# Rebuilding the opening of an attention and SwiGLU kernel: loads ahead of constants, idle matmuls at the start, product with V and row sums ahead of the scores

## The chip, the cores and the metric

The kernel runs on one core of a Trainium2 chip. The metric is the device time of one execution in microseconds (us). A profile is one execution taken by the hardware profiler; its span is about 1.7 us shorter than the time of the same run.

## The reference

Block-sparse attention (4 batches, 8 heads, 768 positions, head size 64) feeds an RMS norm and a SwiGLU layer (3072 tokens, 512 wide, 1536 hidden). Cut to what matters:

```python
scores = (q @ k.T) / sqrt(64)                     # per batch and head
mask = window of one 32-block | first and last block | three sampled blocks per block row
attn = exp(where(mask, scores, -1e9) - max); attn = attn / sum(attn)
x = (attn @ v)                                    # to (3072, 512)
xn = x / sqrt(mean(x * x) + 1e-6) * rms_g
out = (silu(xn @ w_gate) * (xn @ w_val)) @ w_out
```

## The kernel before

A step is one third of a head pair in one half of a batch: two score tiles (128 keys x 2 heads x 384 queries), their exponentials on ScalarE, and the mask multiplications on VectorE. There are 96 steps; the pair n has the steps 3n to 3n+2, and four pairs (12 steps) make a unit u. In step 3n+4 follow the product of the probabilities with V (`av`) and the row sums (`zsum`). When a unit has its four pairs, norm matmuls follow, and then its FFN, cut into pieces of 0.65 us of TensorE time (`ff_g`, `ff_v`, `ff_y`). A loop deals the pieces out to the steps of the next unit: every step earns a credit, `rate`, and each thing placed costs its entry. The order in which the Python emits instructions is the order in each engine's queue. The score tiles share two PSUM buffers (tag "s"), and so does the output of `av` from pair 8 on.

```python
    load_qk(0, 0, 2)                      # q, k of the first pair of heads
    ident = const.tile([P, P], BF16, name="ident")
    nc.vector.memset(ident, 0.0)
    # ... Bm (32x32), Kind (32x768): memsets on VectorE; then on GpSimd ident, jb and seven
    # ... affine_selects that shape Bm and Kind ...
    load_qk(0, 2, 4)
    load_v(0)
    load_qk(0, 4, 8)
    # ... casts and three scalar_tensor_tensors on VectorE put the sampled blocks into Bm ...
    transposes(0, 0)
    # ... Ez, Ew, Sel, SelB, FHL, nhalf on GpSimd ...
    load_w()                              # w_gate, w_val
    # ...
    def qk_mm(n, jt):
        u, pr = divmod(n, NP)
        b, ic = divmod(u, 2)
        if jt == 0:
            ptiles[n] = ppool.tile([P, NC, 2, TG], BF16, name="pt", tag="pt")
        s_ = ps_s.tile([P, 2, 512], FP32, name="s_", tag="s")
        x = qk[b]
        for e in range(2):
            nc.tensor.matmul(
                out=s_[:, e, 0:TG],
                lhsT=x[64 * e:64 * e + 64, 1, jt, pr, :],
                rhs=x[64 * e:64 * e + 64, 0, ic * NT:(ic + 1) * NT, pr, :],
                start=True, stop=True)
        return s_

    def exp_(n, jt, s_):
        nc.scalar.activation(
            out=ptiles[n][:, jt, :, :], in_=s_[:, :, 0:TG], func=AF.Exp, scale=SCALE)

    def mask_(n, jt):
        ic = (n // NP) % 2
        pv = ptiles[n][:, jt]
        nc.vector.tensor_tensor(
            out=pv, in0=pv,
            in1=Mk[:, jt, ic * TG:(ic + 1) * TG].unsqueeze(1).to_broadcast([P, 2, TG]),
            op=ALU.mult)

    def av(n, shared):
        u, pr = divmod(n, NP)
        b = u // 2
        pt_, vb = ptiles[n], vtiles[b]
        if pr == 0:
            osb[u] = opool.tile([P, NP, TG], FP32, name="osb", tag="osb")
            o2s[u] = work.tile([P, NP, TG], BF16, name="o2", tag="o2")
            zwt[u] = ps_a.tile([P, 512], FP32, name="zw", tag="zw")[:, 0:TG]
        if shared:
            o_ = ps_s.tile([P, 2, 512], FP32, name="o_", tag="s")[:, 0, 0:TG]
        else:
            o_ = ps_a.tile([P, 512], FP32, name="oa", tag="acc")[:, 0:TG]
        for jt in range(NC):
            for e in range(2):
                nc.tensor.matmul(
                    out=o_[64 * e:64 * e + 64, :],
                    lhsT=vb[:, 2 * pr + e, jt * D:(jt + 1) * D],
                    rhs=pt_[:, jt, e, :], start=(jt == 0), stop=(jt == NC - 1),
                    skip_group_check=True)
        nc.scalar.copy(out=osb[u][:, pr, :], in_=o_)
        (nc.vector if u == 0 else nc.gpsimd).tensor_tensor(
            out=o2s[u][:, pr, :], in0=osb[u][:, pr, :], in1=osb[u][:, pr, :], op=ALU.mult)

    def zsum(n):
        u, pr = divmod(n, NP)
        pt_ = ptiles[n]
        for j2 in range(NC // 2):
            for e in range(2):
                for par in range(2):
                    c = 2 * e + par
                    nc.tensor.matmul(
                        out=zwt[u][32 * c:32 * c + 32, :], lhsT=Ez[:, pr, :],
                        rhs=pt_[:, 2 * j2 + par, e, :],
                        start=(pr == 0 and j2 == 0), stop=False, skip_group_check=True)

    def ff_g(u, f, wide):
        if f == 0:
            hps[u] = ffw.tile([P, NF, TG], BF16, name="hp", tag="hp", bufs=2)
        if wide:
            gp = ps_s.tile([P, 2, 512], FP32, name="gw", tag="s")[:, 0, 0:TG]
        else:
            gp = ps_f.tile([P, TG], FP32, name="gp", tag="gp")
        for c in range(NP):
            nc.tensor.matmul(
                out=gp, lhsT=wg[:, c, f * P:(f + 1) * P], rhs=xns[u][:, c, :],
                start=(c == 0), stop=(c == NP - 1))
        th = ffw.tile([P, TG], BF16, name="th", tag="th")
        nc.scalar.activation(out=th, in_=gp, func=AF.Tanh, scale=0.5)
        uu = ffw.tile([P, TG], BF16, name="uu", tag="uu")
        nc.vector.scalar_tensor_tensor(
            out=uu, in0=th, scalar=1.0, in1=gp, op0=ALU.add, op1=ALU.mult)
        gst[(u, f)] = uu
    # ... ff_v and ff_y in the same way: four matmuls and a product on VectorE; three matmuls,
    # ... and after every fourth ff_y an output copy on ScalarE and a store ...

    for n in range(NU * NP):
        u, pr = divmod(n, NP)
        s1 = 3 * (n + 1)
        at(s1 + 1, 1.25, av, n, n >= 8)
        at(s1 + 1, 0.7, zsum, n)
        if pr == NP - 1:
            when = (2, 3, 4, 5, 6, 6) if u == 0 else (2, 3, 4, 5, 6, 8)
            at(s1 + when[0], 0.4, norm_a, u)
            at(s1 + when[1], 0.6, norm_b, u)
            at(s1 + when[2], 0.0, norm_c, u)
            at(s1 + when[3], 0.3, norm_d, u)
            at(s1 + when[4], 0.35, norm_e, u, 0)
            at(s1 + when[5], 0.35, norm_e, u, 1)
    for pr in range(1, NP):
        at(3 * (pr - 1) + 1, 0.95, transposes, 0, pr)
    at(1, 0.3, mask_query, 0)
    at(1, 0.3, mask_build, 0, 0, 4)
    at(2, 0.3, mask_build, 0, 4, 6)
    at(5, 0.3, mask_query, 1)
    for i in range(3):
        at(6 + i, 0.3, mask_build, 1, 2 * i, 2 * i + 2)
    for b in range(1, B):
        base = 24 * (b - 1)
        for c in range(NC):
            for i in range(2):
                at(base + (7 + c if b == 1 else 1 + 2 * c + i), 0, load_c, b, i, c)
        for i in range(2):
            at(base + 17, 0, transposes_dma, b, i)
        at(3 * (8 * (b - 1) + (4 if b == 1 else 5)) + 1, 0, load_v, b)
    at(13, 0, load_wo)
    # ...
    while True:
        if step in starts:
            u = starts.index(step)
            queue += ffq[u]
            if u == 0:
                credit = 0.0
        since = 0.0
        todo = fixed.pop(step, ())
        if step < NSTEP:
            n, j = divmod(step, NC // 2)
            sa = qk_mm(n, 2 * j)
            exp_(n, 2 * j, sa)
            sb = qk_mm(n, 2 * j + 1)
            if step < 2:
                exp_(n, 2 * j + 1, sb)
                late += [(n, 2 * j), (n, 2 * j + 1)]
            else:
                for m in late:
                    mask_(*m)
                late = [(n, 2 * j), (n, 2 * j + 1)]
                if queue:
                    since += feed()
                exp_(n, 2 * j + 1, sb)
            credit -= QKT
        else:
            for m in late:
                mask_(*m)
            late = []
        if todo:
            while queue and since < 0.6 and step < NSTEP:
                since += feed()
        tail = 0.0
        for cost, fn, a in todo:
            fn(*a)
            credit -= cost
            if fn in (transposes, norm_d, norm_e):
                tail = 1.2
        while queue and tail > 0 and step < NSTEP:
            c = feed()
            tail -= c
            since += c
        credit -= since
        if u >= 0:
            credit += rate.get(u, 99.0)
            keep = RESERVE if step < NSTEP else 0
            while len(queue) > keep and credit > 0:
                credit -= feed()
            if len(queue) <= keep:
                credit = min(credit, 0.0)
        step += 1
```

The softmax here doesn't subtract the row's maximum and nothing guards it: scores larger than these inputs give would overflow.

Of the kernel before, what the change touches and what calls it, by code (L numbers as in the profile page):

```python
# [17 lines left out]
def kernel(  # L18
# [12 lines left out]
    nc = tc.nc  # L31
# [51 lines left out]
    def load_v(b):  # L83
# [11 lines left out]
    load_qk(0, 0, 2)  # L95


    ident = const.tile([P, P], BF16, name="ident")
    nc.vector.memset(ident, 0.0)
# [6 lines left out]
    nc.gpsimd.affine_select(  # L106
        out=ident, in_=ident, compare_op=ALU.not_equal, fill=1.0,
        base=0, pattern=[[-1, P]], channel_multiplier=1)
# [18 lines left out]
    load_qk(0, 2, 4)  # L127
    load_v(0)
    load_qk(0, 4, 8)

    wg = const.tile([P, DM // P, DFF], BF16, name="wg")
    wv = const.tile([P, DM // P, DFF], BF16, name="wv")
    wo = const.tile([P, NF, DM], BF16, name="wo")
    wgv = moe_w_gate.rearrange("(c p) f -> p c f", p=P)
    wvv = moe_w_val.rearrange("(c p) f -> p c f", p=P)

    def load_w():
        nc.gpsimd.dma_start(out=wg, in_=wgv)
        nc.gpsimd.dma_start(out=wv, in_=wvv)

    def load_wo():
        nc.gpsimd.dma_start(out=wo, in_=moe_w_out.rearrange("(c p) f -> p c f", p=P))

    jbf = const.tile([32, 32], FP32, name="jbf")
    nc.vector.tensor_copy(out=jbf, in_=jb)
    samp_f = const.tile([32, NRND], FP32, name="samp_f")
    nc.vector.tensor_copy(out=samp_f[0:NB, :], in_=samp_i[0:NB, 0:2 * NRND:2])
    nc.vector.memset(Bm[:, 0:1], 1.0)
    nc.vector.memset(Bm[:, NB - 1:NB], 1.0)
    for r in range(NRND):  # L150
        nc.vector.scalar_tensor_tensor(
            out=Bm[0:NB, 0:NB], in0=jbf[0:NB, 0:NB], scalar=samp_f[0:NB, r:r + 1],
            in1=Bm[0:NB, 0:NB], op0=ALU.is_equal, op1=ALU.max)
# [30 lines left out]

    def mask_query(ic):
        cols = slice(ic * TG, (ic + 1) * TG)
        qm = ps_a.tile([32, TG], FP32, name="qm", tag="acc")
        nc.tensor.matmul(
            out=qm, lhsT=Bm[0:NB, :], rhs=Kindf[0:NB, cols], start=True, stop=True)
        nc.vector.tensor_copy(out=Qvis[:, cols], in_=qm)  # L190
# [9 lines left out]

    transposes(0, 0)

# [33 lines left out]
    load_w()  # L236
# [197 lines left out]
    fixed = {}  # L434

    def at(step, cost, fn, *a):
        fixed.setdefault(step, []).append((cost, fn, a))

    for n in range(NU * NP):
        u, pr = divmod(n, NP)  # L440
        s1 = 3 * (n + 1)
        at(s1 + 1, 1.25, av, n, n >= 8)
        at(s1 + 1, 0.7, zsum, n)
        if pr == NP - 1:
            when = (2, 3, 4, 5, 6, 6) if u == 0 else (2, 3, 4, 5, 6, 8)
            at(s1 + when[0], 0.4, norm_a, u)
            at(s1 + when[1], 0.6, norm_b, u)
            at(s1 + when[2], 0.0, norm_c, u)
            at(s1 + when[3], 0.3, norm_d, u)
            at(s1 + when[4], 0.35, norm_e, u, 0)  # L450
            at(s1 + when[5], 0.35, norm_e, u, 1)
    for pr in range(1, NP):
        at(3 * (pr - 1) + 1, 0.95, transposes, 0, pr)
    at(1, 0.3, mask_query, 0)
    at(1, 0.3, mask_build, 0, 0, 4)
    at(2, 0.3, mask_build, 0, 4, 6)
    at(5, 0.3, mask_query, 1)
    for i in range(3):
        at(6 + i, 0.3, mask_build, 1, 2 * i, 2 * i + 2)
    for b in range(1, B):  # L460
        base = 24 * (b - 1)
        for c in range(NC):
            for i in range(2):
                at(base + (7 + c if b == 1 else 1 + 2 * c + i), 0, load_c, b, i, c)
        for i in range(2):
            at(base + 17, 0, transposes_dma, b, i)
        at(3 * (8 * (b - 1) + (4 if b == 1 else 5)) + 1, 0, load_v, b)
    at(13, 0, load_wo)
# [15 lines left out]
    starts = [UST + 7] + [UST * (u + 1) + LAG for u in range(1, NU + 1)]  # L484
    rate = {}
    for u in range(NU):
        lo, hi = starts[u], starts[u + 1]
        need = sum(i[0] for i in ffq[u])
        for st in range(lo, hi):
            need += sum(f[0] for f in fixed.get(st, ())) + (QKT if st < NSTEP else 0)  # L490
        rate[u] = need / (hi - lo)
# [10 lines left out]
    while True:  # L502
# [6 lines left out]
        todo = fixed.pop(step, ())  # L509
        if step < NSTEP:  # L510
# [4 lines left out]
            if step < 2:  # L515
                exp_(n, 2 * j + 1, sb)
                late += [(n, 2 * j), (n, 2 * j + 1)]
            else:
                for m in late:
                    mask_(*m)  # L520
                late = [(n, 2 * j), (n, 2 * j + 1)]
                if queue:
                    since += feed()
                exp_(n, 2 * j + 1, sb)
            credit -= QKT
        else:
            for m in late:
                mask_(*m)
            late = []
        if todo:  # L530
            while queue and since < 0.6 and step < NSTEP:
                since += feed()
        tail = 0.0
        for cost, fn, a in todo:
            fn(*a)
            credit -= cost
            if fn in (transposes, norm_d, norm_e):
                tail = 1.2
# [13 lines left out]
        if step >= NSTEP and not fixed and not queue and u >= NU:  # L552
            break
# [30 lines left out]
```

## Time and profile before

| | |
|---|---|
| time, 3 runs | 363.14 us (363.04 to 363.52) |
| span of the profile | 362.5 us |
| TensorE busy, from 100 to 320 us | over 97% of most stretches (88% from 60 to 100 us) |
| scores of step 18 (unit 0's norm still running) | 51.44 us |
| first FFN matmul | 54.94 us |
| steps 36 to 90, four and a half units | 179.6 us |

The opening is where TensorE is not full. What a matmul costs there depends on TensorE's clock, which the record of the profile shows at full or at half speed ("granted clock" below is its mean share of full speed). These are twelve matmuls of the product with V, and twelve of the row sums, in the timeline of the kernel before (start, length, engine, line, operation):

```profile
19.71 2.13 PE L281 MATMUL oa<-pt,vb 128*64 128x384 bf16 x12
21.78 1.15 PE L297 MATMUL zw<-pt,Ez 128*32 128x384 bf16 x12
...
36.62 1.17 PE L281 MATMUL oa<-pt,vb 128*64 128x384 bf16 x12
37.72 0.67 PE L297 MATMUL zw<-pt,Ez 128*32 128x384 bf16 x12
```

The same work takes 3.3 us at 19.71 and 1.8 us at 36.62: the first pair runs at half clock. Lengths are read together with the PEclk row, since the row has no record before the first change of the clock and shows full speed there.

### The profile page before, as it was taken

How to read it: one execution, taken by the hardware profiler on the slowest of the kernel's cores; microseconds unless marked ns; L12 is line 12 of the kernel's file. 1: busy time of each engine (PE TensorE's matmuls, PEld its weight loads, DVE VectorE, ACT ScalarE, POOL GpSimd, SP SyncE). 2: the span in 40 equal slices, each digit the busy share in tenths (PEclk: the TensorE clock that was granted, in tenths of full speed). 3: DMA queues.
4: the chain of work that ended last, by engine and by line, in shares of the span. 5: the costliest groups of instructions: out<-in, count | busy, mean ns of one | idle time of the engine just before them, and what ended most of it. 6: DMA issues, size and time to landing. Idle time of an engine off the chain costs nothing.

```text
span 362.5 us, 6294 instructions
## 1 busy us (share of the span) xinstructions
PE 333.8 (92%) x2454; PEld 159.1 (44%) x2454; DVE 246.9 (68%) x531; ACT 222.6 (61%) x354; POOL 84.5 (23%) x112
## 2 busy tenths in 40 slices
PE   2787789899799999999999999999999999999995
PEld 1233334344344444455444444454444444555552
DVE  3577786778666786687667785687767776666540
ACT  2465876777676667667666766766676675323321
POOL 8930620135331201143440311021011111100000
PEclk9998988999999999999999999999999999999999
DMA  5999999349661491067770390000000000000012
GB/s 64 171 213 198 157 189 159 72 29 59 44 40 36 104 161 55 32 43 74 73 61 15 62 225 33 32 0 32 29 29 1 31 29 3 30 31 29 33 56 88
DMA packets 69026, 25.58 MB, mean 71 GB/s; under 512 B 57220, under 2 KB 64900, under 8 KB 68996
## 3 DMA queue, kind: packets, MB, share of 16 engines
q0 software_dynamic: 46352, 14.16, 36.9%
q1 hardware_dynamic: 22644, 11.02, 13.0%
q8 instruction: 19, 0.31, 0.4%
q14 instruction: 11, 0.09, 0.1%
HBM read 28.31 MB, written 6.29 MB: 95 GB/s over the span
## 4 chain that ended last, share of the span: by engine, by line
PE 75%; ACT 11%; DVE 7%; issue 4%; DMA 1%; POOL 1%; POOLq 0%; ACTq 0%; DVEq 0%
PE yp L419 16%; PE gp L388 15%; PE vp L405 12%; ACT pt L256 6%; PE zw L297 5%; PE oa L281 3%; ACT th L392 3%; DVE uu L394 2%; DVE pt L262 1%; PE zt L317 1%; DMA kb<-in_k_dram 1%; PE fb L368 1%; DVE xn L373 1%; PE vw L405 1%; PE gw L388 1%
## 5 line engine op out<-in xcount | busy, mean ns | idle before, releaser
L262 DVE TENSOR_TENSOR pt<-pt,Mk 128x768 bf16<-128x768 bf16 x192 | 101.1, 571 | 0.4
L394 DVE SCALAR_TENSOR_TENSOR uu<-th,gp 128x384 bf16<-128x384 bf16 x90 | 49.8, 554 | 61.7 <-ACT th L392 61.4
L388 PE MATMUL gp<-xn,wg 128*128 128x384 bf16 x360 | 74.0, 328 | 3.1 <-DVE uu L394 2.9
L419 PE MATMUL yp<-wo,hp 128*128 128x512 bf16 x288 | 76.1, 380 | 0.0
L392 ACT ACTIVATE th<-gp 128x384 bf16<-128x384 f32 x90 | 44.4, 493 | 49.8 <-PE gp L388 46.8
L405 PE MATMUL vp<-xn,wv 128*128 128x384 bf16 x360 | 73.4, 326 | 0.7 <-DVE hp L408 0.6
L408 DVE TENSOR_TENSOR hp<-uu,vp 128x384 bf16<-128x384 bf16 x90 | 49.6, 551 | 10.2 <-PE vp L405 4.7
L388 PEld LDWEIGHTS <-wg 128*128 128x128 bf16 x384 | 35.5, 98 | 39.4 <-issue 14.5
L405 PEld LDWEIGHTS <-wv 128*128 128x128 bf16 x384 | 35.4, 98 | 29.9 <-issue 9.7
L419 PEld LDWEIGHTS <-hp 128*128 128x128 bf16 x288 | 26.1, 98 | 29.1 <-issue 7.7
L248 PEld LDWEIGHTS <-qkT 64*128 64x128 bf16 x384 | 13.9, 94 | 47.1 <-issue 45.5
L281 PEld LDWEIGHTS <-vb 128*64 128x64 bf16 x384 | 24.5, 115 | 16.8 <-issue 11.1
L425 ACT ACTIVATE yo<-yp 128x512 f32<-128x512 f32 x24 | 14.3, 597 | 13.6 <-PE yp L419 12.1
L297 PE MATMUL zw<-pt,Ez 128*32 128x384 bf16 x384 | 22.6, 344 | 0.0
L373 DVE SCALAR_TENSOR_TENSOR xn<-osb,gcol,fb 128x384 bf16<-128x384 f32 x28 | 15.9, 609 | 8.2 <-PE fb L368 8.2
L79 POOL DMA_DIRECT2D qb<-in_q_dram x18 | 16.4, 909 | 7.7 <-DMA wg<-in_moe_w_gate_dram 7.5
L79 POOL DMA_DIRECT2D qb<-in_k_dram x18 | 16.2, 901 | 7.1 <-DMA wv<-in_moe_w_val_dram 6.5
L332 POOL TENSOR_TENSOR rs<-ms,nhalf 128x3 f32<-128x3 f32 x8 | 7.1, 891 | 39.9 <-DVE ms L329 39.9
L297 PEld LDWEIGHTS <-Ez 128*32 128x32 bf16 x384 | 7.5, 97 | 12.8 <-issue 11.2
L281 PE MATMUL oa<-pt,vb 128*64 128x384 bf16 x96 | 12.6, 413 | 0.2 <-DVE Mk L199 0.2
L287 POOL TENSOR_TENSOR o_3107<-osb 128x384 bf16<-128x384 f32 x4 | 4.1, 1032 | 29.2 <-ACT osb L286 29.2
L287 POOL TENSOR_TENSOR o_2595<-osb 128x384 bf16<-128x384 f32 x4 | 4.1, 1030 | 28.3 <-ACT osb L286 28.3
(556 smaller groups left out, 415.6 us busy)
## 6 DMA issues: line engine op xcount, KB each, us to landing
out_dram<-yo SPq DMA_DIRECT2D x24, 256.0 KB, 2.0
vb<-in_v_dram POOLq DMA_DIRECT2D x4, 768.0 KB, 9.0
qb<-in_q_dram POOLq DMA_DIRECT2D x18, 128.0 KB, 4.5
qb<-in_k_dram POOLq DMA_DIRECT2D x18, 128.0 KB, 4.6
wg<-in_moe_w_gate_dram POOLq DMA_DIRECT2D x1, 1536.0 KB, 14.1
wv<-in_moe_w_val_dram POOLq DMA_DIRECT2D x1, 1536.0 KB, 20.7
wo<-in_moe_w_out_dram POOLq DMA_DIRECT2D x1, 1536.0 KB, 18.5
qb<-in_q_dram POOLq DMA_DIRECT2D x2, 192.0 KB, 3.6
```

The source lines that it names most:

```text
L79: nc.gpsimd.dma_start(out=flat[:, c * DM:(c + 1) * DM].rearrange("p (h d) -> p h d", h=H), in_=src[b, :, :, c * D:(c + 1) * D])
L256: nc.scalar.activation(out=ptiles[n][:, jt, :, :], in_=s_[:, :, 0:TG], func=AF.Exp, scale=SCALE)
L262: nc.vector.tensor_tensor(out=pv, in0=pv, in1=Mk[:, jt, ic * TG:(ic + 1) * TG].unsqueeze(1).to_broadcast([P, 2, TG]), op=ALU.mult)
L281: nc.tensor.matmul(out=o_[64 * e:64 * e + 64, :], lhsT=vb[:, 2 * pr + e, jt * D:(jt + 1) * D], rhs=pt_[:, jt, e, :], start=(jt == 0), stop ...
L297: nc.tensor.matmul(out=zwt[u][32 * c:32 * c + 32, :], lhsT=Ez[:, pr, :], rhs=pt_[:, 2 * j2 + par, e, :], start=(pr == 0 and j2 == 0), stop ...
L373: nc.vector.scalar_tensor_tensor(out=xns[u][:, pr, :], in0=osb[u][:, pr, :], scalar=gcol[:, pr:pr + 1], in1=fb[i], op0=ALU.mult, op1=ALU.mult)
L388: nc.tensor.matmul(out=gp, lhsT=wg[:, c, f * P:(f + 1) * P], rhs=xns[u][:, c, :], start=(c == 0), stop=(c == NP - 1))
L392: nc.scalar.activation(out=th, in_=gp, func=AF.Tanh, scale=0.5)
L394: nc.vector.scalar_tensor_tensor(out=uu, in0=th, scalar=1.0, in1=gp, op0=ALU.add, op1=ALU.mult)
L405: nc.tensor.matmul(out=vp, lhsT=wv[:, c, f * P:(f + 1) * P], rhs=xns[u][:, c, :], start=(c == 0), stop=(c == NP - 1))
L408: nc.vector.tensor_tensor(out=hps[u][:, f, :], in0=uu, in1=vp, op=ALU.mult)
L419: nc.tensor.matmul(out=yp, lhsT=hps[u][:, f, t * P:(t + 1) * P], rhs=wo[:, f, :], start=(f == 0), stop=(f == NF - 1))
```

## The change

The intent is to shorten the opening. The loads of the first batch are issued before the mask constants; TensorE turns eight matmuls of zeros before the first transposes and three after them, so that its clock is up; the work on the mask is moved later; the FFN starts one step earlier. In every step, things marked `pre` (`av`, `zsum`, the first norm matmul) and the masks of the step before are now emitted ahead of the scores, and things marked `mid` behind them. The diff, cut to its core (lines with # in it stand for cuts):

```diff
@@ opening
     load_qk(0, 0, 2)
     ident = const.tile([P, P], BF16, name="ident")
     nc.vector.memset(ident, 0.0)
+    zero = const.tile([P, 512], BF16, name="zero")
+    nc.vector.memset(zero, 0.0)
+    # (ident's affine_select stands here)
+    load_qk(0, 2, 4)
+    load_v(0)
+    load_qk(0, 4, 8)
+    idle = ps_a.tile([P, 512], FP32, name="idle", tag="zw")
+    def spin(k):
+        for _ in range(k):
+            nc.tensor.matmul(
+                out=idle, lhsT=zero[:, 0:P], rhs=zero, start=True, stop=True)
     # ... Bm, Kind ...
-    load_qk(0, 2, 4)
-    load_v(0)
-    load_qk(0, 4, 8)
+    nc.gpsimd.dma_start(out=wg, in_=wgv)
+    nc.gpsimd.dma_start(out=wv, in_=wvv)
     # ... the work on Bm becomes mask_blocks(), called in step 1 ...
+    spin(8)
     transposes(0, 0)
+    spin(3)
@@ placement
-        at(s1 + 1, 1.25, av, n, n >= 8)
-        at(s1 + 1, 0.7, zsum, n)
+        at(pre, s1 + (2 if n == 0 else 1), 1.2, av, n, n >= 8)
+        at(pre, s1 + (2 if n == 0 else 1), 0.7, zsum, n)
         if pr == NP - 1:
-            # norm_a to norm_e at s1 + (2, 3, 4, 5, 6, 6 or 8)
+            at(pre, s1 + 2, 0.35, norm_a, u)
+            # norm_b to norm_e: for u == 0 one step earlier from norm_d on
-    for pr in range(1, NP):
-        at(3 * (pr - 1) + 1, 0.95, transposes, 0, pr)
-    at(1, 0.3, mask_query, 0)
-    at(1, 0.3, mask_build, 0, 0, 4)
-    at(2, 0.3, mask_build, 0, 4, 6)
-    at(5, 0.3, mask_query, 1)
-    for i in range(3):
-        at(6 + i, 0.3, mask_build, 1, 2 * i, 2 * i + 2)
+    for pr, st in ((1, 2), (2, 4), (3, 8)):
+        at(pre, st, 0.95, transposes, 0, pr)
+    at(mid, 1, 0.0, mask_blocks)
+    at(pre, 3, 0.3, mask_query, 0)
+    at(mid, 3, 0.3, mask_build, 0, 0, 6)
+    at(mid, 9, 0.3, mask_query, 1)
+    at(mid, 10, 0.3, mask_build, 1, 0, 6)
-    starts = [UST + 7] + ...
+    starts = [UST + 6] + ...
@@ in the loop
+        if step >= 4:
+            for m in late:
+                mask_(*m)
+            late = []
+        for cost, fn, a in pre.pop(step, ()):
+            fn(*a)
+            credit -= cost
         if step < NSTEP:
             n, j = divmod(step, NC // 2)
             sa = qk_mm(n, 2 * j)
             exp_(n, 2 * j, sa)
             sb = qk_mm(n, 2 * j + 1)
-            # (the masks of the step before stood here)
             if queue:
                 since += feed()
             exp_(n, 2 * j + 1, sb)
     # ... then the things in mid, where all of fixed stood before; the rest as before ...
```

## The prediction

> **What bounds the kernel now.** I read the page's busy tenths and its chain first, then the timeline of the opening (0 to 60 us), then two stretches of the steady part. In the tenths each digit is a fortieth of the span (9.06 us).
>
> ```profile
> PE   2787789899799999999999999999999999999995
> ACT  2465876777676667667666766766676675323321
> PE 75%; ACT 11%; DVE 7%; issue 4%; DMA 1%; POOL 1%; POOLq 0%; ACTq 0%; DVEq 0%
> ```
>
> From about 60 us on, TensorE is full; it also carries three quarters of the chain that ended last. The opening (first six digits, 55 us) is not full. There the chain alternates between a DMA, the mask copies, the exponentials and cold matmuls. The FFN's first matmul starts at 54.94 us. After it, each head pair takes 10.0 us on average (products with V start at 181.08 and 221.07: 40.0 us for four). So a microsecond won before 55 us is a microsecond of the total, and a microsecond of TensorE waiting after it costs a microsecond.
>
> Two timelines decide my answer. First, how one head pair is laid on TensorE in the steady part (start, length, then what):
>
> ```profile
> 179.73 0.34 PE L248 MATMUL s__2321<-qkT 64*128 64x384 bf16 x2
> 179.91 0.33 PE L248 MATMUL s__2325<-qkT 64*128 64x384 bf16 x2
> 180.16 0.82 PE L405 MATMUL vp<-xn,wv 128*128 128x384 bf16 x4
> ...
> 181.08 1.17 PE L281 MATMUL o__2337<-pt,vb 128*64 128x384 bf16 x12
> ...
> 182.18 0.67 PE L297 MATMUL zw<-pt,Ez 128*32 128x384 bf16 x12
> ...
> 182.78 0.34 PE L248 MATMUL s__2365<-qkT 64*128 64x384 bf16 x2
> ```
>
> Two score tiles, one FFN piece (0.65 us of streaming), product with V, row sums, then the next step's scores. Between two steps' scores TensorE has 2.6 us of other work here, and four or five FFN pieces (2.6 to 3.3 us) in the other two steps of a pair. There are two score buffers in PSUM, and ScalarE needs some 1.5 us for a step's two exponentials (0.80 us each, starts 0.71 us apart). So the spacing hides them.
>
> Second, what happens where only little lies between two steps' scores. Before has it once after the FFN starts, with one FFN piece and a short norm matmul between:
>
> ```profile
> 75.97 0.34 PE L248 MATMUL s__992<-qkT 64*128 64x384 bf16 x2
> ...
> 76.41 0.82 PE L388 MATMUL gp<-xn,wg 128*128 128x384 bf16 x4
> ...
> 77.27 0.49 ACT L392 ACTIVATE th<-gp 128x384 bf16<-128x384 f32 x1
> 77.61 0.34 PE L248 MATMUL s__1020<-qkT 64*128 64x384 bf16 x2
> 77.66 0.81 ACT L256 ACTIVATE pt<-s__996 128x768 bf16<-128x768 f32 x1
> ...
> 78.51 0.34 PE L248 MATMUL s__1024<-qkT 64*128 64x384 bf16 x2 [0.57 <-ACT pt L256]
> ```
>
> The second exponential was queued behind the tanh, ended at 78.47, and only then did the fourth score tile get its buffer: it could have followed at 77.78 and came 0.73 us later.
>
> **What the Trainium skill says.** "TensorE: Matmul & The Clock Gate", Part 1, says the array starts at half clock and needs about 3.4 us of sustained activity in a free-running window. The trace agrees: the same twelve matmuls with V take 2.13 us at 19.71 and 1.17 us at 36.62, and the opening is slow until about 23.9 us, after 3.8 us without a gap; it falls back at 27.4, 47.2 and 54.5 us. (The PEclk row shows full clock before 20 us; the durations contradict it.) Part 3 (The mechanism) says matmuls start and end strictly in order, and Part 1 (Architectural detail) that ScalarE and VectorE are strict FIFO. The lines above agree: the stalled score tile held back the FFN matmul behind it, and the exponential stood behind the tanh.
>
> **The change, part by part.**
>
> *Loads earlier.* The first q and k loads are issued at the same time (1.33 and 2.24 us, landing at 5.01 and 6.44), so the first transposes do not move. The next five loads move from 6.17 us to about 3.4 us. The queue pauses now between 6.4 and 8.2 us; the last k half (landing 20.2) comes some 1.8 us sooner, 18.4. The transposes that need it, however, move from the end of step 4 to ahead of step 4's scores, so these scores now wait for it. Weights land some 1.6 us earlier; they are not waited for by TensorE now.
>
> *Idle matmuls.* Eight of 512 columns at half clock (0.43 us each, an estimate: 512 columns at the 1.2 GHz of the same Part 1) fill 1.3 to 4.8 us, when TensorE is idle anyway. Three more after the first transposes sit in the 0.9 us wait for the copies; at half clock they delay the first scores by up to 0.3 us. They may warm the clock early, but step 3 and 4 leave TensorE waiting for some 4 us on mask copies and loads, so I expect the gain to be lost again: under 0.5 us.
>
> *Masks later.* Steps 1 to 2 lose the wait for six mask tiles (step 1 to 2 took 6.07 us against 1.4 us for an exponential-bound step): about 3 us gained there. It comes back at step 3: six copies of 0.5 us, then eight masks of 0.49 us (3.9 us of VectorE) before the first product with V. My count puts step 4's scores at 18.5 to 19.5 us (before 18.58), step 5's at 22.3 to 23.6 (before 24.07). From there on a pair costs 5.3 us as now, the transposes fit under exponentials, the second set of masks costs 2 us in one piece in place of 3.6 us in step 7. The norm and the FFN come one step earlier (step 18 for 19). Step 18's scores at about 51.3 us, against 54.32 for step 19: **-3.0 us**.
>
> *Product with V and row sums ahead of the scores.* It changes nothing in the amount of work. I stepped through the placing loop's bookkeeping by its own costs (order only). In the steady part each pair now reads: V, sums, scores, ONE FFN piece, scores, five pieces, scores, four pieces. The 1.7 us of V and sums no longer lie between those first two steps' scores, but in a gap that was wide enough. With a score at 0: exponentials start at 0.39 and 1.10, the second ends at 1.92, so the fourth score tile starts at 1.96 in place of 1.41 (before, opening: scores at 24.07, fourth at 26.01). That is 0.55 us; with a gate piece the tanh goes ahead of the exponential and it is 1.1 us. Against that, the product with V no longer waits for its own PSUM slot (gap before it 0.16 to 0.27 us, against 0.1 at other switches): -0.1 us. Laid out block by block with the durations above, a unit of four pairs gains +0.4, +0.2 (a norm matmul fills part of the gap), +0.4 and +0.2 (a wait for VectorE of 0.41 us shrinks): 1.2 us a unit. Steps 46 to 95 are 4.2 units: **+5.0 us**. Steps 33 to 45 have a gate piece and an output copy in the gap as well: **+2.2 us**. Steps 18 to 33 in my count take 43.5 us, where before took 40.9 from step 19: **+2.6 us**, a good part of it the step that was not done yet.
>
> Sum: 363.1 - 3.0 + 2.6 + 2.2 + 5.0 = 369.9; I put **369.5 us**. The tail (pure FFN from 325 us) stays.
>
> **Rivals.** (a) *The opening pays and the order is neutral.* The author's reason. For it: TensorE waited only some 8 us in all after 60 us, and a shift within a cycle of three steps looks harmless. Against: the 78.51 line. It would give 358 to 361 us, more if the clock stays high throughout the opening (three half-clock spells of some 3.4 us now). (b) *A new wait in the opening eats its gain*: step 4 on the k load, and fourteen VectorE operations in a row. For it: my own count of steps 4 and 5. Then the opening gives 0 to -1 and the total is 371 to 373. (c) *ScalarE's queue is worse than I count*: in a mixed queue each score wait also delays tanh and thereby VectorE and the FFN banks (the FFN waits for uu, 0.41 us, in some units). Then 2 us a unit, 374 us or more.
>
> **Range and chances.** The two large terms have opposite signs: opening -1 to -5, later +4 to +13. That gives 362 to 376, a shade over 8 in 10. 2% above 363.1 is 370.4, close to my middle, so same and slower are near even: faster 0.08, same 0.50, slower 0.42. Faster needs a neutral order and some 4 us more from the opening than I can find.
>
> **What would show it.** In the changed profile: (1) the first FFN matmul at 51 to 53 us; (2) scores in the step after each product with V waiting "<-ACT pt" for 0.3 to 1.1 us, some 20 times, 9 to 14 us in all among TensorE's waits; (3) products with V four apart by some 41.2 us, not 40.0; (4) TensorE idle between about 14.5 and 18.5 us; (5) the third q/k load landing near 18.4 us; (6) the eight idle matmuls ended before 5.01 us. I am wrong if units still take 40.0 us (then the order is neutral), or if step 18 starts before 49 us (the opening was worth more).

## The result, and the profile after

| | before | after |
|---|---|---|
| time, 4 runs each | 363.33 us (363.04 to 366.17) | 377.19 us (374.49 to 378.2) |
| scores of step 18 | 51.44 us | 57.13 us |
| steps 18 to 36 | 54.6 us | 54.4 us |
| steps 36 to 90 | 179.6 us | 186.2 us |
| steps 90 to 95 | 15.7 us | 16.1 us |
| step 95 to the end of the span | 61.1 us | 62.2 us |

The ratio is 1.0352, with a 95% interval from 1.0276 to 1.0428: slower. (A ratio is the mean time of one kernel's fast runs over that of the other's fast runs of the same rounds, so it is not quite the ratio of the medians.) All the profiles that the argument reads are of the fast state. The rows of the table below the time are from the two profiles, 362.5 and 376.1 us long, and add up to the difference of 13.6 us: 5.7 us in the opening, 8.1 us from step 36 on, and 0.2 us back between them.

Busy tenths, clock and chain of the changed kernel:

```profile
PE   7587788798799899999999999999999998999995
...
PEclk9876669999999999999999999999999999999999
...
PE 70%; ACT 17%; DVE 4%; issue 4%; DMA 3%; POOL 1%; POOLq 0%; ACTq 0%
```

ScalarE's share of the chain went from 11% to 17%: more of the end now hangs on exponentials. The clock row is the second thing to see: 6 and 7 in the slices from 18 to 56 us, where before had 8 and 9.

The product with V now stands ahead of the scores. A steady step of it, in the timeline:

```profile
220.62 0.34 PE L260 MATMUL s__2757<-qkT 64*128 64x384 bf16 x2
...
220.79 0.33 PE L260 MATMUL s__2761<-qkT 64*128 64x384 bf16 x2
...
221.05 0.82 PE L417 MATMUL vp<-xn,wv 128*128 128x384 bf16 x4
...
221.70 0.81 ACT L268 ACTIVATE pt<-s__2761 128x768 bf16<-128x768 f32 x1
221.86 0.34 PE L260 MATMUL s__2773<-qkT 64*128 64x384 bf16 x2
...
222.56 0.34 PE L260 MATMUL s__2777<-qkT 64*128 64x384 bf16 x2 [0.36 <-ACT pt L268]
```

Between the scores at 220.79 and the next step's there is a single FFN piece. The exponential of the second tile ends at 222.51; then, at 222.56, the fourth tile gets its buffer, 1.94 us after the first tile and 0.53 us later than its predecessor at 221.86 would have let it go (scores follow each other by 0.17 us). Between 60 and 320 us TensorE waited for an exponential 28 times, 13.5 us in all; the kernel before waited 5 times, 2.5 us. From step 36 to step 90, where the kernel before has no such wait, there are 14 of them, 6.1 us: nearly all of the 6.6 us that this stretch is longer.

In the opening, between steps 13 and 15, the changed kernel's timeline shows this:

```profile
44.92 0.38 PE L318 MATMUL zw<-o_348,Ew 128*32 128x384 bf16 x4
45.71 1.26 DVE L274 TENSOR_TENSOR pt<-pt,Mk 128x768 bf16<-128x768 bf16 x2 [0.79 <-ACT pt L268]
...
46.89 0.55 DVE L322 COPY zs<-zw 128x384 f32<-128x384 f32 x1
...
47.59 1.43 PE L329 MATMUL zt<-Sel,zs 128*128 128x16 f32 x6 [0.82 <-DVE zs L322]
```

The copy of the sums could have started when the norm matmul ended at 45.3; it stands behind two mask multiplications, which wait for exponentials, and starts at 46.89. TensorE waits for it, and its next matmuls run at half clock (1.43 us; 0.84 us before).

### The profile page after: what moved, and what is told of

The parts are those of the page before. It is cut to its first block, busy times and chain, and to the rows that moved or that the text cites. A ratio compares the mean times of both kernels' runs of the same rounds, so it can differ in the third digit from the quotient of the medians.

```text
span 376.1 us, 6322 instructions
## 1 busy us (share of the span) xinstructions
PE 339.3 (90%) x2465; PEld 159.4 (42%) x2465; DVE 247.7 (66%) x532; ACT 222.1 (59%) x354; POOL 84.2 (22%) x112
## 4 chain that ended last, share of the span: by engine, by line
PE 70%; ACT 17%; DVE 4%; issue 4%; DMA 3%; POOL 1%; POOLq 0%; ACTq 0%
PE gp L400 15%; PE yp L431 15%; ACT pt L268 13%; PE vp L417 11%; PE zw L309 6%; PE oa L293 3%; DMA kb<-in_k_dram 3%; ACT th L404 2%; DVE uu L406 2%; PE zt L329 1%; PE fb L380 1%; PE vw L417 1%; PE gw L400 1%; DVE xn L385 1%; ACT yo L437 1%
## 5 line engine op out<-in xcount | busy, mean ns | idle before, releaser
L404 ACT ACTIVATE th<-gp 128x384 bf16<-128x384 f32 x90 | 44.4, 493 | 55.7 <-PE gp L400 54.0
L260 PEld LDWEIGHTS <-qkT 64*128 64x128 bf16 x384 | 16.8, 95 | 61.6 <-issue 58.7
L293 PEld LDWEIGHTS <-vb 128*64 128x64 bf16 x384 | 20.7, 116 | 19.1 <-issue 11.6
L299 POOL TENSOR_TENSOR o_3103<-osb 128x384 bf16<-128x384 f32 x4 | 4.2, 1052 | 28.3 <-ACT osb L298 28.3
## 6 DMA issues: line engine op xcount, KB each, us to landing
wo<-in_moe_w_out_dram POOLq DMA_DIRECT2D x1, 1536.0 KB, 18.3
```

Of the source, the lines that this page charges most:

```text
L293: nc.tensor.matmul(out=o_[64 * e:64 * e + 64, :], lhsT=vb[:, 2 * pr + e, jt * D:(jt + 1) * D], rhs=pt_[:, jt, e, :], start=(jt == 0), stop ...
```

## The experiments

Sixteen kernels ran, all with a correct result. "Step 18" is the start of that step's first scores in the profile, "36 to 90" the time between the first scores of these steps. Times are medians of all runs; the ratios use fast runs alone (one run of even_pieces, one of back2_loads, three of before_spin and four of back2_fill were slow). The kernel before ran beside each, at 363.4 to 363.9 us.

| kernel | time us | runs | ratio to before (95%) | step 18 | 36 to 90 |
|---|---|---|---|---|---|
| order_back | 370.16 | 4 | 1.0184 (1.0126, 1.0242) | 56.0 | 184.0 |
| order_back2 | 364.84 | 20 | 1.0036 (1.0017, 1.0054) | 53.6 | 179.6 |
| order_only | 379.05 | 4 | 1.0437 (1.037, 1.0505) | 50.6 | 188.0 |
| even_pieces | 366.87 | 20 | 1.0077 (1.0053, 1.0101) | 53.2 | 178.2 |
| warm_after | 383.49 | 4 | 1.0563 (1.0481, 1.0646) | 59.9 | 186.2 |
| fill_free | 379.37 | 4 | 1.0438 (1.0351, 1.0526) | 54.5 | 186.2 |
| back2_fill | 366.38 | 20 | 1.0045 (1.002, 1.0071) | 56.3 | 179.6 |
| masks_mid | 376.88 | 4 | 1.0383 (1.0335, 1.0431) | 54.8 | 186.2 |
| masks_spread | 376.98 | 4 | 1.0379 (1.0332, 1.0426) | 53.9 | 186.2 |
| back2_nospin | 366.29 | 13 | 1.0075 (1.0047, 1.0103) | 53.5 | 179.6 |
| back2_loads | 368.81 | 4 | 1.0105 (1.003, 1.018) | 55.2 | 179.6 |
| mix | 364.20 | 20 | 1.0021 (0.9997, 1.0044) | 53.5 | 179.6 |
| best | 363.93 | 20 | 1.0016 (0.9995, 1.0037) | 53.5 | 180.1 |
| warm_before | 369.22 | 4 | 1.0125 (1.0036, 1.0214) | 55.7 | 179.7 |
| before_spin | 364.25 | 22 | 0.9984 (0.9958, 1.001) | - | - |
| before_even | 363.45 | 22 | 0.9983 (0.9963, 1.0003) | 51.4 | 180.2 |

My theory: the loss from step 36 on is the wait of the scores for the exponential, because one piece lies between two steps' scores. Rival: the order is neutral, and what is lost comes from the opening, directly or through the clock.

### The order taken back: order_back, order_back2

```diff
-        at(pre, s1 + (2 if n == 0 else 1), 1.2, av, n, n >= 8)
-        at(pre, s1 + (2 if n == 0 else 1), 0.7, zsum, n)
+        where = pre if n < 5 else mid
+        at(where, s1 + (2 if n == 0 else 1), 1.25, av, n, n >= 8)
+        at(where, s1 + (2 if n == 0 else 1), 0.7, zsum, n)
# order_back2 also
-            at(pre, s1 + 2, 0.35, norm_a, u)
+            at(pre if u == 0 else mid, s1 + 2, 0.4, norm_a, u)
```

> The changed kernel, with product with V and row sums back behind the scores from the sixth head pair on (step 19); its opening is kept. Theory (the order makes a new wait of the scores for ScalarE): four pairs take 40.0 us again in place of 41.3, the FFN still starts at about 57.5 us, total about 368 to 370 us. Rival (the order is neutral and everything was lost in the opening): total stays at 375 us or more, and four pairs stay at 41.3 us.

It ran at 370.16 us. Steps 36 to 90 took 184.0 us, neither 179.6 nor 186.2. The cause was my edit: the first norm matmul stayed ahead of the scores and so came directly behind the row sums, where it waits for the squares from GpSimd; one pair in four took 10.48 us in place of 9.63.

> As order_back, but the first norm matmul goes back behind the scores too: in order_back it stood directly behind the row sums and waited for the squares from GpSimd (one pair in four took 10.48 us in place of 9.63). Theory: four pairs take 40.0 us as in the kernel before, the opening stays as in the changed kernel (step 18's scores at 56 to 57 us), total 365 to 367 us, so the order alone costs the changed kernel 9 to 11 us and the opening some 2 to 5 us. Rival (order neutral): above 372 us.

With that mended, steps 36 to 90 took 179.6 us, the figure of the kernel before, and the time was 364.84 us: 12.3 us less than the changed kernel (377.19), and 1.4 us more than the kernel before beside it (363.44). Not all of the 12.3 us need be the order's. The edit acts from step 19 on, but the two profiles are 3.5 us apart already at step 18 (57.1 and 53.6 us), where both have run the same instructions (see the clock in the opening, below). From step 18 on they are 9.5 us apart. So the order, together with its entries in the loop, costs about 9.5 us, as far as one profile of each kernel tells.

### The order alone: order_only

The same order, from pair 5 on, in the kernel before.

```diff
-        at(s1 + 1, 1.25, av, n, n >= 8)
-        at(s1 + 1, 0.7, zsum, n)
+        if n < 5:
+            at(s1 + 1, 1.25, av, n, n >= 8)
+            at(s1 + 1, 0.7, zsum, n)
+        else:
+            pre.setdefault(s1 + 1, []).append((1.2, av, (n, n >= 8)))
+            pre[s1 + 1].append((0.7, zsum, (n,)))
@@ in the loop, ahead of the scores
+        for cost, fn, a in pre.pop(step, ()):
+            fn(*a)
+            credit -= cost
```

> The kernel before, with product with V and row sums ahead of the scores from the sixth head pair on; its opening is kept. Theory: FFN start unchanged at about 54.9 us, four pairs take 41.3 us, total 363.3 + 7 to 10 = 370 to 373 us. Rival (order neutral): 363 to 364 us.

379.05 us: the rival is out, and the loss of 15.5 us is larger than I expected. Part of that is a place that I had not seen. Around steps 31 to 33 no FFN piece is left to deal, and TensorE has little to do. In this profile (interval, its length, busy TensorE, weight loads, VectorE, ScalarE, GpSimd with counts, then the granted clock, DMA share, GB/s):

```profile
96.00:98.00 2.00, 1.04 (x6) 0.37 (x5) 1.31 (x4) 1.41 (x3) 1.72 (x2) 0.79 1.01 65
98.00:104.00 6.00, 5.87 (x19) 2.53 (x19) 2.12 (x5) 1.69 (x4) 0.00 (x0) 0.50 0.69 44
```

The clock fell to half and stayed there for nearly 7 us of full work; steps 33 to 36 took 14.1 us against 10.8. The kernel before has no such spell there.

### The same order with the pieces dealt evenly: even_pieces

```diff
-        at(pre, s1 + (2 if n == 0 else 1), 1.2, av, n, n >= 8)
-        at(pre, s1 + (2 if n == 0 else 1), 0.7, zsum, n)
+        at(pre, s1 + (2 if n == 0 else 1), 0.0, av, n, n >= 8)
+        at(pre, s1 + (2 if n == 0 else 1), 0.0, zsum, n)
```

> The changed kernel with the order kept (product with V and row sums ahead of the scores in every step), but their cost entered as 0 in place of 1.2 and 0.7 in the loop that deals out FFN pieces: each step then gets about three pieces, and two to four of them stand between the scores of an AV step and those of the next, not one. The work is the same. Theory (the loss is the score tile that waits for the second exponential because only one piece lies ahead of it): steps 36 to 90 take 179.5 to 182 us again in place of 186.2, total 366 to 369 us. Rival (AV ahead costs in itself, by PSUM slots or the clock): 374 us or more.

366.87 us. The product with V still stands ahead of the scores, and yet a unit of four pairs takes 39.9 us (products with V at 218.37 and 258.28), as in the kernel before (40.0), in place of 41.3. In its timeline two pieces lie between the steps:

```profile
210.52 0.34 PE L260 MATMUL s__2745<-qkT 64*128 64x384 bf16 x2
...
210.95 0.82 PE L431 MATMUL yp<-wo,hp 128*128 128x512 bf16 x3
...
211.61 0.81 PE L400 MATMUL gp<-xn,wg 128*128 128x384 bf16 x4
...
212.53 0.33 PE L260 MATMUL s__2771<-qkT 64*128 64x384 bf16 x2
```

The fourth tile comes 2.01 us after the first, and waits for nothing. From step 36 to 90 TensorE waits for an exponential 6 times, 2.6 us, in place of 14 times, 6.1 us. (That this stretch took 178.2 us, 1.4 us less than before, is no gain: one piece fewer was dealt there, and the time from step 90 to the end grew by 2.2 us.) From step 36 to the end of the span it is 257.2 us, against 256.4 in the kernel before and 264.5 in the changed kernel. So of the 8.1 us the order with evenly dealt pieces keeps 0.7; the rest came from the order and two cost entries together. The entries only tell the loop how to deal: with 1.9 entered for an AV step (a step with the product with V), the loop gave it one piece and the other two steps four or five. The kernel before deals in the same way (it enters 1.95) and does not wait, because there V and the sums lie beside that one piece. Even dealing in the old order was not run. What even_pieces loses against order_back2 (2.0 us) is at the ends: steps 33 to 36 take 12.3 us against 10.8, with a half clock there, steps 90 to 95 take 16.8 us against 15.7, and the rest 62.3 us against 61.4.

### The clock in the opening: warm_after, fill_free, back2_fill, warm_before

The four kernels with the changed opening and no edit to it (after, order_back, order_back2, even_pieces) are a test by themselves. Their instructions on TensorE, VectorE and ScalarE are the same up to the first FFN matmul. Yet step 18 came at 57.1, 56.0, 53.6 and 53.2 us, and up to there the clock record of the four shows 27.3, 23.9, 20.0 and 18.3 us at half speed. The two rows of the kernel before, of the changed kernel and of order_back2 for 30 to 44 us:

```profile
30.00:37.00 7.00, 4.95 (x60) 2.15 (x60) 5.63 (x12) 4.10 (x7) 0.68 (x1) 0.96 1.61 187
37.00:44.00 7.00, 5.17 (x62) 2.06 (x58) 4.63 (x10) 5.99 (x10) 5.60 (x7) 1.00 2.42 154
```

```profile
30.00:37.00 7.00, 5.88 (x35) 2.12 (x36) 3.68 (x8) 3.33 (x6) 2.78 (x4) 0.53 2.06 168
37.00:44.00 7.00, 5.89 (x28) 1.83 (x31) 5.69 (x12) 3.37 (x6) 3.50 (x4) 0.50 2.14 162
```

```profile
30.00:37.00 7.00, 5.08 (x43) 2.03 (x44) 6.03 (x13) 3.77 (x7) 3.49 (x4) 1.00 2.07 167
37.00:44.00 7.00, 5.86 (x40) 1.87 (x38) 4.28 (x9) 4.71 (x8) 2.77 (x3) 0.51 2.16 169
```

The last figure but two is the granted clock: full in both rows before, half in both after, and full then half in order_back2. The changed kernel has the fewest matmuls in these stretches (63, against 122 before) and the longest busy time. What this costs shows from step 5 to step 18, in the same order:

```profile
24.07:51.44 27.37, 21.25 (x197) 9.04 (x193) 21.87 (x51) 20.18 (x30) 9.03 (x10) 0.88 1.62 183
```

```profile
22.76:57.13 34.37, 27.06 (x201) 10.61 (x198) 22.51 (x50) 21.43 (x31) 9.03 (x10) 0.69 1.56 184
```

```profile
22.78:53.60 30.82, 23.69 (x201) 9.05 (x198) 23.00 (x50) 21.43 (x31) 9.00 (x10) 0.78 1.60 188
```

TensorE is idle (length less busy time) for 6.1, 7.3 and 7.1 us, and busy for 21.3, 27.1 and 23.7 us with about the same number of matmuls. So of the 7.0 us that the changed kernel takes longer here than the kernel before, 1.2 us are waiting and 5.8 us longer matmuls; and of the 3.6 us between it and order_back2, which run the same instructions, 3.4 us are longer matmuls. The clock moves the opening by some 3.5 us from one execution to another. To see what a full clock would win, I put idle matmuls (zeros, results never read) into the opening.

```diff
# warm_after (512 columns, into the bank with tag "gp"), steps 4 to 17; warm_before alike, steps 0 to 18
             exp_(n, 2 * j, sa)
+            if 4 <= step < 18:
+                fill(1)
             sb = qk_mm(n, 2 * j + 1)
+            if 4 <= step < 18:
+                fill(1)
# and fill(2) behind each mask matmul (warm_before: 1)
```

> The changed kernel, with idle matmuls (512 columns, zeros, into a free PSUM bank, never read) put after each score tile of steps 4 to 17 and after each mask matmul, so that TensorE is never idle for long in the opening. Theory A (the opening is long because the clock falls to half from 17 to 24, 31 to 44 and 48 to 54 us): the clock stays full from about 10 us, the FFN starts at 52 to 54 us in place of 57.6, total 371 to 374 us. Theory B (the opening is long because mask copies and masks stand in one piece on VectorE, the clock is a symptom): FFN start within 1 us of 57.6, total 376 to 378 us.

> The kernel before, with the eight and three idle matmuls at the start and one idle matmul after each score tile of steps 0 to 18 and each mask matmul; no other change. If half clock costs the opening time (cold until 23.9 us, 27.4 to 30.7, 47.7 to 51.2 us): FFN start at 51 to 53 us, total 360 to 362 us. If the opening is bound by ScalarE, VectorE and loads alone: 363 us or, where the idle matmuls get in the way, up to 365.

Both misses: 383.49 and 369.22 us, longer than their bases. The idle matmuls took a bank which the transposes' copies must release first, and these stand in VectorE's queue behind the masks. In warm_after:

```profile
22.35 0.59 PE L256 MATMUL fl<-zero 128*128 128x512 bf16 x1 [2.87 <-DVE qkT L169]
```

A filler that waits is no filler, so these two say nothing of the clock. In fill_free and back2_fill the idle matmuls have 128 columns and go to columns 384 to 511 of the row sums' bank, which are never read and wait for nothing.

```diff
# fill_free, on the changed kernel; back2_fill, on order_back2: 3 and 2, and 20 in place of 12, none at the mask matmuls
+    def fill(k):         # back2_fill starts at step 5
+        for _ in range(k):
+            nc.tensor.matmul(
+                out=bank["t"][:, 384:512], lhsT=zero[:, 0:P], rhs=zero[:, 0:P],
+                start=bank["t"] is idle, stop=False, skip_group_check=True)
+            fill(3)     # behind each score tile of steps 4 to 17, not 14 and 15
+            fill(4)     # behind each mask matmul
+            fill(12)    # between the two halves of the third transposes
```

> The changed kernel with idle matmuls of 128 columns in the opening that wait for nothing: they go to columns 384 to 511 of the bank of the row sums, which nobody reads (in warm_after the idle matmuls took a bank whose release waited for VectorE, and held TensorE up). Three after each score tile of steps 4 to 17 (not 14 and 15), four after each mask matmul, twelve in the wait for the k load. Theory A (half clock costs the opening its time): clock full for most of 17 to 54 us, step 18 at 52 to 55 us, total 371 to 375. Theory B (VectorE's queue and loads set the opening): step 18 stays at 56 to 58 us although the clock is full.

> As order_back2, with idle matmuls of 128 columns into unread columns, only where TensorE waits for ScalarE or the k load: three after the first and two after the second score tile of steps 5 to 17 (not 14 and 15), twenty in the wait for the k load; none among the mask matmuls, where fill_free paid for them. Theory A (half clock is what the rebuilt opening loses): full clock from 20 to 47 us, step 18's scores at 50.5 to 52.5 us in place of 53.6, total 362 to 364 us. Theory B (VectorE, ScalarE and the order of the opening set it): step 18 within 1 us of 53.6 although the clock is full, total 364 to 366.

In fill_free the clock was full from 19.2 to 46.5 us, and step 18 came at 54.5 us, inside the 53.2 to 57.1 of the kernels without fillers; step 10, where the fillers stand among the mask matmuls, took 4.6 us (3.1 to 3.9 us without them). back2_fill did not hold the clock in every run: its 16 fast runs spread from 362.79 to 367.93 us, longer the lower the clock, and four more (to 372.16 us) count as slow. The six with a mean clock of 0.985 or more average 364.2 us; the 20 runs of order_back2, at 0.96 to 0.98, average 365.0 us. So with the clock nearly full, and the fillers paid for, the kernel gained 0.8 us. What a full clock without fillers would win no run shows; idle matmuls of this kind do not win it safely.

### VectorE's queue in the opening: masks_mid, masks_spread

```diff
# masks_mid: in steps 4 to 18 the masks go behind the second score tile again
-        if step >= 4:
+        if step >= 19:
             for m in late:
                 mask_(*m)
             late = []
@@ behind sb = qk_mm(...)
+            if 4 <= step < 19:
+                for m in late:
+                    mask_(*m)
+                late = []
# masks_spread
-    at(mid, 10, 0.3, mask_build, 1, 0, 6)
+    for i in range(3):
+        at(mid, 10 + i, 0.3, mask_build, 1, 2 * i, 2 * i + 2)
```

> The changed kernel with the mask multiplications of steps 4 to 18 behind the second score tile of a step, as before, in place of ahead of everything in the step. Theory (in VectorE's queue the masks, which wait for ScalarE, stand ahead of the copies that TensorE waits for: transposes, zs): step 15's and step 18's scores come 1.5 to 3 us sooner than in the changed kernel (57.1), total 373.5 to 375.5 us. Rival (the half clock makes it): step 18 within 1 us of 57, total 376 to 378.

> The changed kernel with the second set of six mask tiles built two a step in steps 10 to 12, not all six in step 10. Theory (the lump holds TensorE and ScalarE for 2.4 us): step 11 comes some 2 us sooner, step 18 one to two us sooner, total 375 to 376. Rival (what is saved at step 11 is paid in steps 12 and 13, VectorE being the limit there): no change within 1 us.

376.88 and 376.98 us, against 377.19: no gain in the time that four runs could show. (Step 18 came at 54.8 and 53.9 us, but the unedited opening had 53.2 to 57.1.) In the profiles the steps in question are shorter (step 14 took 1.75 us in masks_mid, 2.6 in order_back2 and 3.2 in the changed kernel; step 10 took 1.2 us in masks_spread, against 3.1 and 3.9). But the next steps give it back: step 12 of masks_spread took 6.1 us, in order_back2 4.3. Moving one wait of this chain uncovers the next.

### The winning parts: back2_nospin, back2_loads, before_spin

```diff
# back2_nospin, on order_back2
-    spin(8)
     transposes(0, 0)
-    spin(3)
# back2_loads, on order_back2: load_qk(0, 2, 4), load_v(0), load_qk(0, 4, 8) behind the constants again
# before_spin: the kernel before with zero, idle, spin(8) and spin(3), and nothing else
```

> As order_back2, without the eight and three idle matmuls at the start. If they matter: the first scores and transposes run at half clock (0.50 us a score tile in place of 0.34), step 2 comes up to 1 us later, and the total rises by 0.3 to 1 us above 364.8. If not: 364 to 365.5 us, because step 4 waits for the k load anyway.

> As order_back2, but the second to fifth load of q, k and v are issued behind the mask constants again, as in the kernel before. If the load of the last k half sets step 4 (it landed at 18.1 us): step 4's scores come some 2 us later than 18.9 us, total 366 to 367. If VectorE's masks set the pace from there: total within 0.5 us of 364.8.

> The kernel before with nothing but the eight and three idle matmuls at the start (one part of the change alone). back2_nospin ran about 1.3 us longer than order_back2, so up to 1 us shorter than the kernel before, 362.5 to 363.5 us, is expected. If the first scores wait for q, k and the mask anyway: no difference, 363.5 to 364.

Without the idle matmuls order_back2 takes 366.29 us, with the loads behind the constants 368.81 us (four runs, 365.2 to 371.0, the longest of them slow). Neither is well clear of the noise: the ratios to the kernel before are 1.0047 to 1.0103 and 1.003 to 1.018, that of order_back2 itself 1.0017 to 1.0054. So about 1.4 us for the idle matmuls is likely in this opening, and a gain from the loads is not shown by the times. In the profile of back2_loads step 4 comes at 20.45 us in place of 18.88. In the kernel before, the idle matmuls alone make no difference that 22 runs show (0.9984, interval from 0.9958 to 1.001). Its profiled run was of the slow state and is not read.

### Towards a better version: mix, best, before_even

```diff
# mix, on order_back2: masks_spread, and
-        at(where, s1 + (2 if n == 0 else 1), ...)
+        at(where, s1 + (3 if n == 0 else 1), ...)
-    for pr, st in ((1, 2), (2, 4), (3, 8)):
+    for pr, st in ((1, 2), (2, 5), (3, 8)):
# best, on mix; before_even, on before_spin: av and zsum of pairs 11 to 27 ahead of the scores, cost 0
```

> As order_back2, with the second mask set two tiles a step (steps 10 to 12), the third pair's transposes one step later (step 5, when its k load is nearer) and the first product with V one step later (step 6). Meant to be the best version: step 4 at about 15.5 us, step 18 at 51 to 53 us, total 361 to 364. If the opening is bound by VectorE and the clock instead: 364 to 366.

> As mix, and in the middle (head pairs 11 to 27) product with V and row sums ahead of the scores with their cost entered as 0, as in even_pieces, whose steps 36 to 90 took 178.2 us against 179.6 us in the kernel before. Expected: the opening of mix (364.2 us in all), less 0.5 to 1.5 us: 362.8 to 364 us, the same as the kernel before or up to 0.3% below it. If the change of order at its two ends makes new waits: 364.5 to 366.

> As before_spin, and for head pairs 11 to 27 product with V and row sums ahead of the scores with cost 0, so that each step gets about three FFN pieces. best had 1 to 2 us less between steps 36 and 90 this way. Expected 361.5 to 363.5 us; if the change at the two ends of the stretch costs what the middle saves: 363.5 to 365.

mix gets step 4 at 16.6 us and step 5 at 19.3 us, 2.3 and 3.4 us ahead of order_back2, and has lost it by step 13 (42.1 against 42.0 us). At 364.20 us it is not told apart from the kernel before; nor are best (363.93 us, beside 363.94) and before_even (363.45 us, beside 363.79; interval from 0.9963 to 1.0003). No version that I ran beats the kernel before beyond its noise. The expectation of before_even says that best had 1 to 2 us less between steps 36 and 90; its profile has 180.1 us there, 0.5 us more than mix. What even dealing in the middle wins between steps 33 and 36 (9.7 us against 10.8, in both) is paid back later: from step 36 to the end both take 257.8 us, the kernel before 256.4.

## Why the prediction was wrong, point by point

- **The range** ended at 376 us; 377.19 was measured, and slower was given 0.42. Of the two large terms the order had the right mechanism and the right size; the opening had the wrong sign.
- **The step that failed** is "Step 18's scores at about 51.3 us, against 54.32 for step 19: -3.0 us". The profile has 57.1 us, and the three other profiles of the same opening 56.0, 53.6 and 53.2. The -3.0 us sets step 18 against step 19 of the kernel before; step 18 against step 18 (51.4 us) the forecast was -0.1 us, and +5.7 us came (+1.7 to +4.5 in the other three). The table shows that nearly the whole miss is there (the forecast of a stretch is the profile before with the forecast's +2.2 and +5.0 us put in):

| stretch | forecast | changed kernel | before |
|---|---|---|---|
| to step 18 | 51.3 us | 57.1 us | 51.4 us |
| 18 to 33 | 43.5 us | 43.0 us | 43.8 us |
| 33 to 46 | 46.7 us | 48.6 us | 44.5 us |
| 46 to 95 | 166.7 us | 165.1 us | 161.7 us |
| 95 to the end | 61.1 us | 62.2 us | 61.1 us |

- Up to step 5 its working held: step 4 at 18.87 us (forecast 18.5 to 19.5), step 5 at 22.76 (22.3 to 23.6), with the wait for the k load and the mask copies where they were put. What failed is "From there on a pair costs 5.3 us as now". From step 5 to step 18 the forecast has 28.3 us, the profiles 30.8 (order_back2) to 34.4 us; the products with V of pairs 1 to 4 follow each other by 7.0, 9.6 and 8.0 us in the changed kernel. The 5.3 us were read where the product with V took 1.17 us, at full clock (36.62 us in the kernel before). In the changed kernel those of pairs 2, 3 and 4 took 2.13 us each, and the norm's matmuls waited 0.82 us for a copy behind the masks. What the runs show in place of the 5.3 us is above all half clock: over the kernel before, 5.8 us of longer matmuls and 1.2 us of waiting from step 5 to step 18.
- The remark that "I expect the gain to be lost again" was right for the first spell, from 17 to 24 us. That the two later spells could grow was not in the forecast at all; rival (b) had a new wait in the opening, but at 371 to 373 us.
- **The order**, with its entries, was forecast right. From step 18 on the forecast has 318.0 us, the profile 318.9, the kernel before 311.1. The mechanism is shown by three runs: away with order_back2, there in the other opening with order_only, and nearly away with even_pieces, which keeps the order and changes the dealing. In a unit it took 41.27 us (products with V at 218.92 and 260.19), forecast 41.2; the fourth tile came 1.94 us after the first, forecast 1.96. That the whole sum fits so well is in part luck: steps 33 to 46 were 1.9 us longer than forecast and steps 46 to 95 1.6 us shorter, and the end grew by 1.1 us, where the forecast said "The tail (pure FFN from 325 us) stays". A half clock around step 33 adds to it in some executions (order_only, even_pieces).
- Of the six signs, (2) 28 waits (for some 20) and 13.5 us, (3), (5) a k load at 18.08 us, and (6), the idle matmuls over at 4.94 us, came as said; (4) came in part, with TensorE busy for 1.8 us of 14.5 to 18.5 us; (1), the first FFN matmul at 51 to 53 us, did not: 57.56.
- **What stays open**: why the clock falls where it does, and so why steps 5 to 18 have 11.5 to 21.3 us of half clock in the four profiles of the changed opening and 6.8 us in the kernel before. Whether the waits behind VectorE's queue bring the clock down was not separated, since each edit moved both.

## What to carry to other kernels

Before you move work within a repeating cycle, write down for every consumer with few buffers how much other work lies between two of its uses, before and after; a sum over the cycle does not show a gap of 0.65 us where 1.5 us of exponentials must fit. A cost entry of a loop that deals out filler work is as much a part of the schedule as the order: here, with the new order, two of them were worth 10 us (377.19 us to 366.87). An opening gained at one step is gained only if the chain behind it was not set by something else: read the step times up to the point where the steady part begins, not the first wait that vanishes. And read busy and idle time apart: here, from step 5 to step 18, the waits grew by 1.2 us and the busy time by 5.8 us.

## What the Trainium skill lacked or had wrong

- "TensorE: Matmul & The Clock Gate", Part 1: the page speaks of sustained activity, and of idle time for the fall to half clock. In the changed kernel TensorE was busy for 11.8 of the 14 us from 30 to 44 us and was at half clock for 13.6 of them; in the kernel before it was busy for 10.1 of the same 14 us at nearly full clock. Busy time in a trace, itself longer at half clock, does not tell the state; the page lacks how busy a window must be.
- The same page and part calls the ramp less than 1% of a typical span and not worth fitting. That is said of the ramp, and this case adds what later falls of the clock cost: in the 47 fast runs of the kernel before that ran beside even_pieces, the time went from 361.5 to 365.9 us as the mean clock went from 0.990 to 0.974 (a line through them: 2.2 us for each 0.01), so 1.2% in all; and the same instructions took 53.2 to 57.1 us to step 18. The spells are multiples of 3.41 us, which agrees with the page's window.
- No page has a rule for the work between two uses of a double buffer; the runs show 1.94 us from the first tile of a step to the first free buffer of the second tile of the next (two exponentials of 0.81 us, 0.70 us apart).
